# Fourteen places of a split operand, on one byte modulo 256 or on fourteen

## The chip, the core and the metric

The kernel runs on one core of one Trainium2 chip. The metric is the device time of one execution in microseconds; the median of several runs is given.

## What is computed

The input x has 2048 rows of 576 features. Two branches read it, an attention with memory and a gated feed-forward network, and a gate of x mixes them:

```
g = sigmoid((x * gate_w).sum(-1))
a = A(x, wq, wk, wv, wo, beta)      # 32 heads of 18, four segments of 512 rows:
                                    # causal softmax in a segment, mixed with a
                                    # running memory phi(k)^T v of the segments before
b = (silu(x @ w_gate) * (x @ w_up)) @ w_down      # 4608 hidden features
out = g * a + (1 - g) * b
```

## The kernel before

All large products are made of 4-byte operands that are split in two: a high part, rounded on ScalarE to the matmul's 4-byte format, and a low part, the difference, made on VectorE (`split`, lines 114 to 116). A product of two split matrices is three matmuls: high by high, high by low, low by high. TensorE loads one operand, 128 x 128, as weights and streams the other, up to 512 columns, past it.

The work comes in three stages.

The first stage (to about 225 us) runs over the four segments. For each, `qk` makes queries and keys by `products` (line 138): fourteen matmuls of 512 columns, in which weights of `qhi` and `qlo` are loaded and x's split parts stream. `v_step` makes the values by the same `products` with the parts exchanged: x's split parts are loaded as weights, and rows of `vw` stream.

The second stage (to about 1700 us) runs twice over 36 tiles of the hidden features, once for two of the segments and once for the other two. For a tile and two segments it needs gate and up projections; these are done with seven block products in place of eight (Strassen's scheme in Winograd's form), so seven calls of `seven(t, j)` for a tile. A call of `seven` is six matmuls of line 1034, with weights of a tile `wo_` and a stream of 512 columns of x's split part number j, and one of line 1037 for the last 64 features, with weights `rh` and the stream `xr`. There are 2 x 36 x 7 = 504 calls. Between the calls, `tick` and `beat` put other work: `down_group` (line 893, the down projection: streams of 320 or 256 columns of `dw`), and steps of the attention (lines 727 and 769 for the scores, 748 for a transposition, 798 and 800 for probabilities times values), all by a written order of steps.

The third stage multiplies the attention's result by wo (line 138 again, `wo` streams) and mixes the branches.

x's split operands lie in a pool `xo`, which is opened after the constants. It has fourteen places `x_slot(j, z)`, j from 0 to 6 and z 0 or 1, each with a high and a low part of 512 elements: [128, 2, 512] of 4 bytes, 4096 bytes in each partition. Place number n is 2j + z. In the first stage a segment's x lies in four of them, and the others serve as room for loads (`staging`): x's chunks, the weights of queries, keys and values, masks. Before the second stage the fourteen are filled with the seven combinations of x's blocks, two feature blocks each, `XO[j][z]` in place `SLOT[j]`, z; between the passes they are filled anew. In the third stage eight of them take loads of the feed-forward result. The same pool holds seven tiles `xr` of 2048 bytes.

Since 4096 and 2048 are multiples of 256, all fourteen places begin on the same byte modulo 256. Tiles `wo_` are 2048 bytes. The order of a call:

```
for z in range(2):
    for p, q in ((0, 0), (0, 1), (1, 0)):
        nc.tensor.matmul(t, w[:, p, z], x[z][:, q], ...)
nc.tensor.matmul(t, rem[:, RPOS[j]], XR[j], ...)
```

All DMAs are issued from SyncE (`nc.sync.dma_start`). The program reserves a ring for descriptors of dynamic DMAs in SBUF, here 1024 bytes (`dynamic_dma_scratch_size`, line 1221).

Of the kernel before, what the change touches and what calls it, by code (L numbers as in the profile page):

```python
# [20 lines left out]
P = 128  # L21
# [4 lines left out]
L = 512  # L26
# [27 lines left out]
RPOS = (0, 1, 4, 2, 5, 6, 3)  # L54
BLOCKS = {3: (4, 5), 6: (6, 7), 9: (8, 9), 12: (10, 11), 15: (12,), 18: (13,), 21: (14,), 24: (15,), 27: (16,), 30: (17,)}
KR = 6 * DH


def f32(ap):
# [4 lines left out]
def gated_mix(ctx, tc, xT, xrest, wf, wfr, wfh, wd, wv, wo, beta, cmask, ident, bmask, out):  # L64
    nc = tc.nc
    ctx.enter_context(tc.manual_schedule())

    def pool(st, name, bufs, side="left", space=None):
        if space is None:
            return st.enter_context(tc.tile_pool(name=name, bufs=bufs, side=side))  # L70
        return st.enter_context(tc.tile_pool(name=name, bufs=bufs, space=space))
# [24 lines left out]
    xo = pool(ctx, "xo", 1)  # L96
# [43 lines left out]
                mid()  # L140

    def x_slot(j, z, dtype=F32R):
        return xo.tile([P, 2, L], dtype, name=f"xo{j}{z}")

    def xr_tile(j, dtype=F32R):
        return xo.tile([P, L], dtype, name=f"xr{j}")
# [15 lines left out]
    def staging():  # L162
        return x_slot(*next(turns), F32).rearrange("p a b -> p (a b)")
# [11 lines left out]
    def stack_loads(u):  # L175
# [5 lines left out]
        for pr in range(2):  # L181
# [6 lines left out]
            if pr == 0:  # L188
                r += [(tq[5 * DH:KR], q[:, :, 2]), (tk[5 * DH:KR], k[:, :, 0])]
        return r  # L190

    def row_load(u):
        nc.sync.dma_start(qst[u % NST][KR:KR + 3].rearrange("z j (i n) -> z (j i) n", n=P), mxd[u])

# [75 lines left out]
    with ExitStack() as st:  # L270
# [18 lines left out]
        def x_tiles(s):  # L289
            j = 5 * (s % 2)  # L290
            return [x_slot(j + kt // 2, kt % 2) for kt in range(4)], xsp.tile([P, L], F32R, name="xs")
# [24 lines left out]
        def trio():  # L316
            ts = [first_tile() for _ in range(3)]
            xk, xs = xs_of[0]
            for kt in range(NT):
                nc.scalar.activation(qw[0][0][0][:, kt], qraw[kt][:, 0], AF.Copy)  # L320
                raw = xr[kt]
                if kt < 4:
                    split(xk[kt][:, 0], xk[kt][:, 1], raw)
                else:
                    xs_split(xs, raw)
                for m in range(3):
                    if m:
                        nc.scalar.activation(qw[m][0][0][:, kt], qraw[kt][:, m], AF.Copy)
                    nc.vector.tensor_sub(qw[m][1][0][:, kt], qraw[kt][:, m], f32(qw[m][0][0][:, kt]))
                for p, q in ((0, 0), (0, 1), (1, 0)) if kt < 4 else ((0, 0), (1, 0)):  # L330
                    for m in range(3):
                        nc.tensor.matmul(ts[m], qw[m][p][0][:, kt], xk[kt][:, q] if kt < 4 else xs,  # L332
                                         start=(kt == 0 and p + q == 0), stop=(kt == 4 and p == 1))
            return ts
# [128 lines left out]
        for kt in range(NT):  # L463
            if kt % 2 == 0:
                both = staging(), staging()
            a = both[0][:, L * (kt % 2):L * (kt % 2) + 3 * P].rearrange("p (m n) -> p m n", n=P)
# [14 lines left out]
        first = trio()  # L481
# [42 lines left out]
        def first_split(j, z):  # L524
            XO[j][z] = x_slot(SLOT[j], z)
            split(XO[j][z][:, 0], XO[j][z][:, 1], rx[{1: (0, z), 4: (1, z), 2: (1, 2 + z), 6: (0, 2 + z)}[j]])
# [155 lines left out]
    with ExitStack() as st:  # L682
# [37 lines left out]
        def s_bank(u, n):  # L720
# [4 lines left out]
            for c, pr, i in bank:  # L725
                w = P * (i + 1)
                nc.tensor.matmul(t[:, c:c + w], qs[:KR, pr, P * i:P * i + P], ks[:KR, pr, 0:w],  # L727
                                 start=True, stop=True)
# [34 lines left out]
        def t_bank(u, k):  # L763
            qs, ks = qst[u % NST], kst[u % NST]
            t = ts_tile()
            for pr, j in TPLAN[k]:
                _, c = blk(pr, j, j)
                w = L - P * j
                nc.tensor.matmul(t[:, c:c + w], ks[:KR + 3, pr, P * j:P * j + P], qs[:KR + 3, pr, P * j:L],  # L769
                                 start=True, stop=True)  # L770
# [271 lines left out]
        for pos, (half, f) in enumerate(seq):  # L1042
# [45 lines left out]
            a, y, xx = a_tile(), y_tile(), x_tile()  # L1088
# [63 lines left out]
        for n in range(17):  # L1152
# [6 lines left out]
            if n:  # L1159
                tt = order[n - 1]  # L1160
                ff = ffs.pop(n - 1)
                for hf in range(2):
                    c = slice(288 * hf, 288 * hf + 288)
                    t = chain_tile()
# [67 lines left out]
```

## Time and profile before

| what | value |
|---|---|
| median of 3 runs | 1804.82 us (1804.8 to 1804.99) |
| span of the profiled execution | 1803.0 us |
| TensorE busy | 1779.1 us, 99% |
| weight loads busy | 1529.7 us, 85% |
| VectorE, ScalarE, GpSimd busy | 1269.7, 960.0, 832.3 us |
| mean granted TensorE clock | 0.997 |
| DMA queue share | 60.3% |

The profile is one execution. Its page gives the span, from the first to the last instruction; the runs' times are 1.8 us above it. Busy time is the time in which an engine had an instruction under way; a matmul's length reaches to the modelled end of its pipeline, so lengths overlap, and the distance from one start to the next says more of the rate than a length does.

### The profile page before, as it was taken

To read this page: it belongs to the slowest core of one execution; us is meant where nothing else is said; L and a number is where in the kernel's file an instruction comes from. 1 tells how busy PE (TensorE), PEld (TensorE's weight loads), DVE (VectorE), ACT (ScalarE), POOL (GpSimd) and SP (SyncE) were. 2 spreads that over 40 slices of the span, in tenths; PEclk is the share of its full clock that TensorE was granted. 3 is DMA by queue.
4 is the path that set the end of the run, shared out by engine and by line. 5 is a ranking of instruction groups with operands and counts; after the bars stand their busy time and mean duration, and the time that the engine had idled before them with its cause. 6 is when DMAs were issued, how large, how long until landed. Compare 5 with 4: busy or idle time off the path is not lost.

```text
span 1803.0 us, 36363 instructions
## 1 busy us (share of the span) xinstructions
PE 1779.1 (99%) x12444; PEld 1529.7 (85%) x12444; DVE 1269.7 (70%) x3257; ACT 960.0 (53%) x1799; POOL 832.3 (46%) x1065
## 2 busy tenths in 40 slices
PE   9999999999999999999989999999999999999999
PEld 7898978888888888888877888888887887888899
DVE  6566566778877777777777767777777777764455
ACT  7666564465556555655546465355355355354511
POOL 4434632345554455345535555555555555553121
PEclk9999999999999999999999999999999999999999
DMA  8643496777657756776478456466455455456644
GB/s 289 215 174 141 148 324 205 229 260 264 186 198 248 256 181 193 246 247 193 160 262 247 137 176 195 135 172 195 124 179 181 144 168 180 137 160 187 199 137 139
DMA packets 244073, 352.01 MB, mean 195 GB/s; under 512 B 83440, under 2 KB 125680, under 8 KB 243888
## 3 DMA queue, kind: packets, MB, share of 16 engines
q1 hardware_dynamic: 243888, 349.68, 60.3%
q8 instruction: 99, 1.62, 0.4%
q14 instruction: 86, 0.70, 0.1%
HBM read 210.72 MB, written 138.87 MB: 194 GB/s over the span
## 4 chain that ended last, share of the span: by engine, by line
PE 92%; DVE 2%; DMA 2%; ACT 2%; issue 1%; SPq 0%; POOL 0%; ACTq 0%; DVEq 0%
PE bank L1034 36%; PE bank L893 25%; PE bank L138 11%; PE bank L1037 6%; PE bank L769 4%; PE bank L727 4%; PE bank L798 2%; PE bank L800 1%; PE bank L446 1%; PE bank L400 1%; DMA wo__23682<-wc 0%; DVE xo L116 0%; DMA stk<-q 0%; PE bank L332 0%; DMA raw<-in_xT_dram 0%
## 5 line engine op out<-in xcount | busy, mean ns | idle before, releaser
L893 PE MATMUL bank<-dw,hh 128*128 128x320 f32 (+1 forms) x2304 | 486.5, 304 | 6.0 <-DVE ya L898 4.4
L863 POOL TENSOR_TENSOR p<-pe,p 128x512 f16<-128x512 f32 x320 | 382.7, 1196 | 155.5 <-DVE p L861 107.1
L893 PEld LDWEIGHTS bank<-dw,hh 128*128 128x128 f32 x2304 | 377.9, 189 | 24.8 <-DVE ya L898 6.3
L773 ACT ACTIVATE pe<-bank 128x512 f32<-128x512 f32 x320 | 190.3, 595 | 313.9 <-PE bank L769 285.5
L893 PE MATMUL bank<-dw,hl 128*128 128x320 f32 (+1 forms) x1152 | 340.2, 295 | 0.3 <-DVE hl L116 0.3
L781 POOL TENSOR_SCALAR_AFFINE_SELECT pe<-pe 128x256 f32<-128x256 f32 (+1 forms) x320 | 137.5, 430 | 293.7 <-ACT pe L773 289.8
L734 DVE CUSTOM_DVE_ANT_0 scr<-bank,cm 128x512 bf16<-128x512 f32 (+3 forms) x512 | 247.8, 484 | 20.0 <-PE bank L727 12.0
L898 DVE TENSOR_TENSOR ya<-bank,ya 128x320 f32<-128x320 f32 x352 | 157.9, 453 | 113.2 <-PE bank L893 110.8
L893 PEld LDWEIGHTS bank<-dw,hl 128*128 128x128 f32 x1152 | 217.6, 189 | 0.9 <-DVE hl L116 0.9
L1037 PE MATMUL bank<-xr,rh 128*128 128x512 f32 x504 | 196.8, 391 | 0.0
L861 DVE CAST p<-pe 128x512 f16<-128x512 f32 x320 | 152.3, 476 | 0.0
L769 PE MATMUL bank<-qst,kst 111*128 111x512 bf16 (+3 forms) x512 | 150.9, 303 | 0.0
L727 PE MATMUL bank<-kst,qst 108*128 108x512 bf16 (+3 forms) x512 | 126.0, 300 | 0.6 <-DVE mb L734 0.5
L247 POOL TENSOR_TENSOR ws<-raw 128x256 f32<-128x256 f32 x72 | 66.2, 920 | 108.0 <-DMA raw<-in_wf_dram 51.7
L977 DVE TENSOR_TENSOR hl<-row,hh 128x512 fp32r<-128x512 f32 x120 | 99.7, 831 | 18.9 <-ACT hh L976 18.4
L1037 PEld LDWEIGHTS bank<-xr,rh 128*128 128x128 f32 x504 | 94.7, 188 | 20.3
L1101 ACT ACTIVATE row<-bank 128x512 f32<-128x512 f32 x72 | 43.1, 599 | 122.3 <-PE bank L1037 122.3
L1106 DVE TENSOR_TENSOR row<-bank,row 128x512 f32<-128x512 f32 x72 | 49.8, 691 | 81.8 <-ACT bank L1105 81.8
L1116 DVE TENSOR_TENSOR row<-bank,row 128x512 f32<-128x512 f32 x72 | 49.7, 690 | 64.2 <-PE bank L1037 51.5
L1105 ACT ACTIVATE bank<-bank 128x512 f32<-128x512 f32 x72 | 41.9, 582 | 97.9 <-PE bank L1037 94.8
L138 PE MATMUL bank<-xo,qhi 128*128 128x512 f32 x264 | 83.1, 396 | 0.0
L1098 DVE TENSOR_TENSOR bank<-bank,row 128x512 f32<-128x512 f32 x72 | 50.2, 697 | 41.6 <-PE bank L1037 33.4
(1702 smaller groups left out, 4040.3 us busy)
## 6 DMA issues: line engine op xcount, KB each, us to landing
rh<-rc SPq DMA_DIRECT2D x72, 336.0 KB
dc<-dw SPq DMA_DIRECT2D x36, 576.0 KB
dw<-dc SPq DMA_DIRECT2D x36, 576.0 KB
raw<-in_wf_dram SPq DMA_DIRECT2D x72, 256.0 KB
stk<-q SPq DMA_DIRECT2D x32, 384.0 KB
draw<-in_wd_dram SPq DMA_DIRECT2D x36, 288.0 KB
rc<-rt SPq DMA_DIRECT2D x42, 224.0 KB
vd<-vps SPq DMA_DIRECT2D x8, 912.0 KB
```

What stands on the lines that cost most here:

```text
L138: nc.tensor.matmul(t, st[n], mv[n], start=(n == 0), stop=(n == 13))
L727: nc.tensor.matmul(t[:, c:c + w], qs[:KR, pr, P * i:P * i + P], ks[:KR, pr, 0:w], start=True, stop=True)
L734: nc.vector.tensor_tensor_reduce(scr[:, :w], t[:, c:c + w], cm[:, L - w:L], 1.0, -3.0e38, OP.add, OP.max, m[:, k:k + 1])
L769: nc.tensor.matmul(t[:, c:c + w], ks[:KR + 3, pr, P * j:P * j + P], qs[:KR + 3, pr, P * j:L], start=True, stop=True)
L773: nc.scalar.activation(pe, t, AF.Exp, scale=SCALE)
L781: nc.gpsimd.affine_select(d, d, pattern=pat, compare_op=OP.is_ge, fill=0.0, base=0, channel_multiplier=-1)
L861: nc.vector.tensor_copy(p1, pe)
L863: nc.gpsimd.tensor_sub(p2, pe, p1)
L893: nc.tensor.matmul(t, p, q[:, cs], start=(n == 0), stop=(n == 3 * CH - 1))
L898: nc.vector.tensor_add(ya[:, i, cs], t, ya[:, i, cs])
L1034: nc.tensor.matmul(t, w[:, p, z], x[z][:, q], start=first and n == 0, stop=False, skip_group_check=True)
L1037: nc.tensor.matmul(t, rem[:, RPOS[j]], XR[j], start=False, stop=True, skip_group_check=True)
```

## The change

Each place gets padding, so that the fourteen begin on given bytes from the pool's beginning, beside the 4096 bytes of each place before it. The table `HOME` has these bytes; a tile is made larger by whole 32 bytes, and the remainder is an offset within it. The last entry, 768, is the sum of the padding. The ring of descriptors becomes 768 bytes smaller, 256 in place of 1024.

```
+HOME = (0, 40, 64, 128, 160, 216, 232, 264, 304, 352, 456, 504, 528, 544, 768)
...
     def x_slot(j, z, dtype=F32R):
-        return xo.tile([P, 2, L], dtype, name=f"xo{j}{z}")
+        n = 2 * j + z
+        first, after = HOME[n] // 32 * 32, HOME[n + 1] // 32 * 32
+        t = xo.tile([P, 2 * L + (after - first) // 4], dtype, name=f"xo{j}{z}")
+        a = HOME[n] % 32 // 4
+        return t[:, a:a + 2 * L].rearrange("p (a b) -> p a b", a=2)
...
-    nc = _bacc.Bacc("TRN2", target_bir_lowering=False, num_devices=1, dynamic_dma_scratch_size=1024)
+    nc = _bacc.Bacc("TRN2", target_bir_lowering=False, num_devices=1, dynamic_dma_scratch_size=256)
```

## The prediction

> **What bounds the kernel now.** I read the page first: the share of each engine, the DMA queues, the chain that ended last.
>
> ```profile
> span 1803.0 us, 36363 instructions
> ...
> PE 1779.1 (99%) x12444; PEld 1529.7 (85%) x12444; DVE 1269.7 (70%) x3257; ACT 960.0 (53%) x1799; POOL 832.3 (46%) x1065
> ...
> q1 hardware_dynamic: 243888, 349.68, 60.3%
> q8 instruction: 99, 1.62, 0.4%
> q14 instruction: 86, 0.70, 0.1%
> ...
> PE 92%; DVE 2%; DMA 2%; ACT 2%; issue 1%; SPq 0%; POOL 0%; ACTq 0%; DVEq 0%
> PE bank L1034 36%; PE bank L893 25%; PE bank L138 11%; PE bank L1037 6%; PE bank L769 4%; PE bank L727 4%; PE bank L798 2%; PE bank L800 1%; PE bank L446 1%; PE bank L400 1%; DMA wo__23682<-wc 0%; DVE xo L116 0%; DMA stk<-q 0%; PE bank L332 0%; DMA raw<-in_xT_dram 0%
> ```
>
> TensorE is busy 99% of the span and is 92% of the chain; line 1034, whose moving operand is x's split tile `xo`, is the largest part, 36%. So the time follows the pitch (start to start) of matmuls, and little else. The span is 1803.0 us, the median of the runs 1804.82 us: 1.8 us lie around the span, and I carry them over unchanged.
>
> Next the timeline of TensorE, for that pitch: columns are start, length from the first start to the last end, engine, line, operands, shape, count.
>
> ```profile
> 500.58 1.29 PE L1034 MATMUL bank<-xo,wo__6057 128*128 128x512 f32 x5
> 501.71 0.39 PE L1037 MATMUL bank<-xr,rh 128*128 128x512 f32 x1
> 501.94 1.52 PE L1034 MATMUL bank<-xo,wo__6070 128*128 128x512 f32 x6
> 503.30 0.39 PE L1037 MATMUL bank<-xr,rh 128*128 128x512 f32 x1
> 503.53 0.39 PE L1034 MATMUL bank<-xo,wo__6085 128*128 128x512 f32 x1
> ...
> 505.55 0.46 PE L893 MATMUL bank<-dw,hh 128*128 128x320 f32 x2
> 505.84 0.31 PE L893 MATMUL bank<-dw,hl 128*128 128x320 f32 x1
> 505.99 0.31 PE L893 MATMUL bank<-dw,hh 128*128 128x320 f32 x1
> ...
> 507.25 0.40 PE L893 MATMUL bank<-dw,hh 128*128 128x256 f32 x2
> 507.49 0.28 PE L893 MATMUL bank<-dw,hl 128*128 128x256 f32 x1
> 507.61 0.28 PE L893 MATMUL bank<-dw,hh 128*128 128x256 f32 x1
> ```
>
> One call of `seven` is seven products, from 501.94 to 503.53: 1.59 / 7 = 227 ns each, no idle time between. Three products of 320 columns take 505.99 - 505.55 = 0.44 us, 147 ns each; three of 256 take 0.36, 120 ns each. The difference, 27 ns for 64 columns, is 0.417 ns for a column. So 512 columns account for 213.3 ns, 320 for 133.3 and 256 for 106.7, and each of the three widths carries about the same rest: 13.8 (the row's 10 ns stand behind it), 13.3, 13.3. I use 13.3, and 226.7 ns for the pitch at 512. The change can act on that rest alone, and only where it depends on the byte at which an operand starts.
>
> Does it depend on that? Two more places of the timeline.
>
> ```profile
> 507.97 1.55 PE L1034 MATMUL bank<-xo,wo__6092 128*128 128x512 f32 x6
> ...
> 208.09 1.74 PE L138 MATMUL bank<-vw,xo 128*128 128x288 f32 x12
> 209.67 0.43 PE L138 MATMUL bank<-vw,xs 128*128 128x288 f32 x2
> 209.94 0.83 PE L446 MATMUL bank<-Mm,ph 128*128 128x152 f32 x6
> ...
> 1101.65 0.38 PE L727 MATMUL bank<-kst,qst 108*128 108x512 bf16 x1
> 1101.87 0.27 PE L769 MATMUL bank<-qst,kst 111*128 111x256 bf16 x1
> ```
>
> The six products at 507.97, the first after another kind of matmul, span 1.55 us where the six at 501.94 span 1.52: the same code, operands on the same bytes, so the rest also has a memory of what went before and takes some products to settle. The fourteen products of `v_step` from 208.09 to 209.94 have moving operands that start on other bytes: a row of `vw` is 290 elements, 1160 bytes, so its five chunks begin on 0, 136, 16, 152 and 32 modulo 256, and the low halves on others. They take 1.85 / 14 = 132.1 ns; their 288 columns account for 120, so the rest is 12.1 where the products on one byte carry 13.3. And a bf16 product of 512 columns has a pitch of 0.22 us, a rest of 5 to 7 ns. The rest is thus no fixed cost of the array; it is smaller for other operands, and only a little smaller where 4-byte operands are spread.
>
> **The change part by part.** Nothing is added or removed in instructions; the matmuls, loads, copies and DMAs are the same in number and order. Three things move.
>
> *The byte of the moving operand.* Each place of `xo` was 4096 bytes, so all fourteen began on one byte modulo 256. Now they begin 0, 40, 64, 128, 160, 216, 232, 8, 48, 96, 200, 248, 16 and 32 bytes further modulo 256 (the table, reduced). The places grow by 768 bytes in all, which is what the ring gives up, and 768 is three times 256: every other tile keeps its byte modulo 256, and the products of lines 893, 798, 800, 727 and 769 keep theirs. Touched are 504 calls of `seven` (line 1037 has one product in each, x504 on the page):
>
> ```profile
> L1037 PE MATMUL bank<-xr,rh 128*128 128x512 f32 x504 | 196.8, 391 | 0.0
> ...
> L138 PE MATMUL bank<-xo,qhi 128*128 128x512 f32 x264 | 83.1, 396 | 0.0
> ...
> L138 PE MATMUL bank<-xo,qlo 128*128 128x512 f32 x132 | 51.6, 391 | 0.0
> ```
>
> That is 6 x 504 = 3024 products of line 1034 and 396 of line 138, 3420 with `xo` as moving operand, of 12444. Bounds for one: at best the rest falls to that of the bf16 product, 13.3 to about 5, a gain of 8 ns, 27 us over all. At worst no product ever settles, because each meets another pair of bytes than the one before: the 1.55 us span has five pitches and one length of 0.39, (1.55 - 0.39) / 5 = 232 ns, 5.3 ns above 226.7, 18 us over all. The nearest row is that of `v_step`, also 4-byte operands, a moving operand on changing bytes and weights on one: 12.1, a gain of 1.2 ns. I take that: 3420 x 1.2 = **-4.1 us**.
>
> A rule of the Trainium skill speaks against any effect: "TensorE: Matmul & The Clock Gate", section "Step-by-step: what each phase is for", says that TensorE reads SBUF through two independent ports, one for the streamed operand and one for the weights, so that a weight load takes no read bandwidth from the running matmul. By it the bytes could not matter to this pair and the term would be nothing; the trace's 12.1 against 13.3 does not bear that out fully, but does not refute it either, since widths and weights differ there as well.
>
> *The settling.* The second pass has 252 calls of `seven`, most of them behind other matmuls. One that settles costs 0.03 us more (1.55 against 1.52), so at most 252 x 0.03 = 7.6 us are in it, and fewer, since some calls follow one another. If the pitch differs from product to product anyway, the slow run after a switch should lose its regular form; I take the unsettled part as two thirds of that, 5 us, and credit half of it, **-2.5 us**, with ends at 0 and -7.6.
>
> *Loads into the places.* x's chunks, the weights of the first stage and, at the end, the attention's partner `ffd` are loaded by DMA into places of `xo` that start off 32 or 64 bytes now.
>
> ```profile
> 2.31 4.90 DMA xo<-in_xT_dram
> ...
> xo<-in_xT_dram SPq DMA_DIRECT2D x20, 256.0 KB
> ```
>
> One such load is on the chain, 4.90 us at the start; the others lie beside TensorE, which waits for them nowhere in its list of waits. Between nothing and a tenth of that load: **+0.2 us**, ends 0 and +0.5. The Trainium skill, "DMA: Bandwidth & Descriptors", section "How a descriptor splits into AXI transactions", says that a transfer which does not begin on 256 bytes pays one more transaction; for a row of 2048 bytes that is nine in place of eight, by which this load would be an eighth longer, an estimate of 0.6 us. No row of this trace shows a load off its alignment.
>
> *The ring.* All but 185 of the packets are on the queue `hardware_dynamic`, the 185 are instructions, and all DMAs are issued on SP; no queue of GpSimd appears. The ring of descriptors is in use by none of them: 0, and there is no row by which a smaller one could cost.
>
> ACT's and DVE's copies into the places keep shape and count; the engines are at 53% and 70%, and hide a few ns each behind TensorE; without that cover a copy of 16 in the first stage would cost its own lengthening only. Sum: -4.1 - 2.5 + 0.2 = -6.4 us. Span 1796.6, time **1798.4 us**. For this case alone I give 1789 to 1801: the settling and the rest between one half of and twice what I took, and somewhat beyond.
>
> **The rivals.**
>
> *Never settled (slower).* On one byte the products reach 227 ns and stay there for dozens of calls; that steady pitch is a property of a relation that repeats, and with fourteen bytes it never repeats for more than three products. Then the mean is the unsettled 232 ns. The first pass, mostly settled now, loses most. For it: 1.55 against 1.52 with equal bytes. Against it: `v_step` changes bytes at almost every product and is not slower. Price: 5.3 x 3420 = 18 us less the 5 us that are unsettled already: +13 us, 1818 us, from 1809 to 1823. It decides if the mean pitch of the calls that follow one another passes 228 ns.
>
> *No effect.* The rest of 13.3 ns belongs to the weight load's hand-over and not to bytes; the three widths with equal rests speak for it. Time 1804.8, within 0.2% (3.6 us, 1 ns a product), which is about what a measurement of this kernel can tell from no change.
>
> *The collision goes.* The rest falls to the bf16 product's 5 to 7 ns in most products: 3420 x 7 = 24 us, 1781 us. For it: that row. Against it: `v_step`, spread and still at 12.1. By the rule "Back-to-back issue gap" of the same page of the Trainium skill, N / 2.4 + 2.5, the pitch could be 215.8 ns; no 4-byte product here comes near it.
>
> **How the numbers follow.** Forecast (modest gain) 0.43, collision goes 0.09, no effect 0.19, never settled 0.29. Faster by over 0.2%: 0.43 + 0.09 = 0.52; within: 0.19; slower: 0.29. The range leaves out the collision case below 1784 (0.09) and the upper end of the slower case above 1821 (about 0.1): 1784 to 1821.
>
> **What would show it.** In settled calls of the first pass: six products of line 1034 and one of 1037 spanning on the mean under 1.58 us (1.59 now), with single pitches no longer all equal; 1.60 or more is the slower rival, an unchanged 1.59 everywhere the rival of no effect, 1.54 the collision that goes. `v_step`'s fourteen at 1.85 us should move less than 0.03, lines 893 at 147 and 120 ns not at all; if those move too, the byte of `xo` is not what acts. DVE, ACT and POOL busy sums should stay within 1%. The forecast is wrong if the mean pitch of line 1034 in the first pass is unchanged or higher while the time still falls, or if a wait for a DMA into `xo` shows on TensorE.

## The result, and the profile after

The changed kernel is slower: 1819.27 us median of three runs (1816.74 to 1819.37) against 1804.82, a ratio of 1.0076 with a 95% interval from 1.006 to 1.0093, or +14.45 us. The profiled execution of the changed kernel took 1819.27 us itself, 1817.5 us of it span. Three executions among those of the experiments below were slow (one of e1_ring, one of e6_one and one of the kernel before beside e4_both), and the medians here leave them out. The lines of code have moved up by one to five numbers there: 1034, 1037, 893 and 138 are now 1039, 1042, 898 and 139.

The page of the changed kernel: the span, busy time of each engine, and the chain that ended last. PE is TensorE, PEld its weight loads, DVE VectorE, ACT ScalarE and POOL GpSimd.

```profile
span 1817.5 us, 36363 instructions
...
PE 1796.2 (99%) x12444; PEld 1534.4 (84%) x12444; DVE 1271.3 (70%) x3257; ACT 960.6 (53%) x1799; POOL 832.4 (46%) x1065
...
PE 92%; DVE 3%; ACT 1%; DMA 1%; issue 1%; POOL 1%; SPq 0%; DVEq 0%; ACTq 0%; POOLq 0%
```

The instructions are as many as before, and DVE, ACT and POOL are as busy as before to 0.2%. TensorE alone has grown, from 1779.1 to 1796.2 us. So the time is lost in TensorE's matmuls. The `...` in the block stands for lines left out, here and below. The timeline of TensorE of the changed kernel (start, length, engine, line, operands, shape, count), in calls of `seven` shortly ahead of those shown of before, and in the same call of `v_step`:

```profile
498.25 1.58 PE L1039 MATMUL bank<-xo,wo__5964 128*128 128x512 f32 x6
499.67 0.39 PE L1042 MATMUL bank<-xr,rh 128*128 128x512 f32 x1
499.89 1.56 PE L1039 MATMUL bank<-xo,wo__5970 128*128 128x512 f32 x6
501.29 0.39 PE L1042 MATMUL bank<-xr,rh 128*128 128x512 f32 x1
501.52 1.56 PE L1039 MATMUL bank<-xo,wo__5986 128*128 128x512 f32 x6
...
209.91 1.75 PE L139 MATMUL bank<-vw,xo 128*128 128x288 f32 x12
211.51 0.42 PE L139 MATMUL bank<-vw,xs 128*128 128x288 f32 x2
211.77 0.82 PE L451 MATMUL bank<-Mm,ph 128*128 128x152 f32 x6
```

From 498.25 to 499.89 and on to 501.52 are 1.64 and 1.63 us for seven products, 1.59 before. Most calls look like this: among the calls of both passes that stand between other calls the median is 1628 ns, against 1587 before, so 232.6 ns a product in place of 226.7. The products no longer settle at 226.7; most starts are 224 to 238 ns apart, and the same pattern comes back in tile after tile. The products with 288 columns, which load `xo` as weights, take 1.86 us for fourteen, 1.85 before.

The same by groups of instructions (busy time, mean ns of one, idle before), the changed kernel first and then the kernel before:

```profile
L898 PE MATMUL bank<-dw,hh 128*128 128x320 f32 x1152 | 265.2, 317 | 5.1 <-DVE ya L903 3.7 <-ACT hh L116 1.3
L898 PE MATMUL bank<-dw,hh 128*128 128x256 f32 x1152 | 224.9, 291 | 0.8 <-DVE ya L903 0.7
L1042 PE MATMUL bank<-xr,rh 128*128 128x512 f32 x504 | 197.9, 393 | 0.0
L139 PE MATMUL bank<-xo,qhi 128*128 128x512 f32 x264 | 84.0, 399 | 0.0
L139 PE MATMUL bank<-xo,qlo 128*128 128x512 f32 x132 | 52.2, 395 | 0.0
```

```profile
L893 PE MATMUL bank<-dw,hh 128*128 128x320 f32 x1152 | 265.0, 316 | 5.2 <-DVE ya L898 3.7 <-ACT hh L115 1.4
L893 PE MATMUL bank<-dw,hh 128*128 128x256 f32 x1152 | 224.5, 291 | 0.8 <-DVE ya L898 0.7
```

The down projection, whose operands did not move against each other, costs the same. The queries' and keys' products with `xo` (`qhi`, `qlo`) have grown by 0.9 and 0.6 us, and the rest is line 1039. Summed from each start to the next, line 1034/1039 went from 715.6 to 728.5 us (+13.0) and the 432 products of x's places with `qhi` and `qlo` (lines 138 and 332, now 139 and 337) from 101.3 to 102.9 (+1.6): together 14.6 us, as much as the whole loss.

### The profile page after: what moved, and what is told of

It reads as the page before. It is cut to its first block, busy times and chain, and to the rows that moved or that the text cites. A ratio compares the mean times of both kernels' runs of the same rounds, so it can differ in the third digit from the quotient of the medians.

```text
span 1817.5 us, 36363 instructions
## 1 busy us (share of the span) xinstructions
PE 1796.2 (99%) x12444; PEld 1534.4 (84%) x12444; DVE 1271.3 (70%) x3257; ACT 960.6 (53%) x1799; POOL 832.4 (46%) x1065
## 3 DMA queue, kind: packets, MB, share of 16 engines
q8 instruction: 99, 1.62, 0.4%
## 4 chain that ended last, share of the span: by engine, by line
PE 92%; DVE 3%; ACT 1%; DMA 1%; issue 1%; POOL 1%; SPq 0%; DVEq 0%; ACTq 0%; POOLq 0%
PE bank L1039 37%; PE bank L898 24%; PE bank L139 10%; PE bank L1042 6%; PE bank L774 4%; PE bank L732 4%; PE bank L803 2%; PE bank L805 1%; PE bank L405 1%; DVE xo L117 1%; PE bank L451 1%; PE bank L337 1%; DMA stk<-q 0%; PE bank L957 0%; DMA raw<-in_xT_dram 0%
```

## The experiments

All edits are against the changed kernel unless the text says otherwise; ratios are to the kernel before on the same chip. The experiments were made on the view that in the kernel before all operands of the 4-byte 512-column products, streams (`xo`, `xr`) and weights (`wo_`, `rh`, `qhi`, `qlo`) alike, lie on one byte modulo 256, and that the change moved the streams `xo` alone. No trace holds addresses; the runs bear it out, since the kernel's products settle at the pitch that equal bytes have in m1_bytes, and moving `xo`, `xr` or `rh` alone by 128 bytes costs time.

**e1_ring: the small ring, without the fourteen bytes.**

```
-HOME = (0, 40, 64, 128, 160, 216, 232, 264, 304, 352, 456, 504, 528, 544, 768)
+HOME = 14 * (0,) + (768,)
```

> The ring of 256 bytes alone: the table is fourteen zeros and 768, so the padding lies behind the last place, all fourteen places stay on one byte modulo 256, and all other tiles are where the changed kernel has them. Theory 'change of byte' (a product settles at a pitch of 227 ns while the starting bytes of its operands repeat, and every change of byte from one product to the next throws it off): 1804.8 us, pitch 227 ns. Rival 'relation to the weights' (x off the byte of its weights costs by itself, repeated or not): 1804.8 too. Rival 'ring' (the smaller ring or the moved constants cost): about 1819.

Measured: 1803.72 us against 1803.71; 1.0002 [0.9992, 1.0011]. The ring and the shift of the constants cost nothing; the loss is in the bytes.

**e2_shift: all fourteen on one byte, but another one than the weights'.**

```
+    xo.tile([P, 32], F32, name="gap2")
...
+HOME = 14 * (0,) + (640,)
```

> All fourteen places on one byte, but 128 bytes from the byte of the weights, of xr and of the rest (a tile of 128 bytes ahead of the first place, 640 behind the last). 'Change of byte': the six products of a call repeat their relation, and only the product with xr differs, so two changes in seven products: between 1804.8 and 1812. 'Relation to the weights': 3420 products pay, as much as with fourteen bytes or more: 1819 or above. Rival 'fine alignment' (only starts off a multiple of 32 bytes cost): 1804.8.

Measured: 1814.18 us; 1.0059 [1.0044, 1.0074], +10.5 us. The time lies between the two expectations. Here nothing differs from product to product in the six, yet nearly three quarters of the loss are there. Timeline of TensorE of this kernel:

```profile
495.13 1.55 PE L1040 MATMUL bank<-xo,wo__5971 128*128 128x512 f32 x6
496.52 0.39 PE L1043 MATMUL bank<-xr,rh 128*128 128x512 f32 x1
496.75 1.54 PE L1040 MATMUL bank<-xo,wo__5987 128*128 128x512 f32 x6
```

1.62 us a call; the median of the calls that stand between others is 1623 ns, 231.9 ns a product. It is not the variety of bytes alone that costs.

**e3_by32: fourteen different bytes, all multiples of 32.**

```
+HOME = tuple(range(0, 448, 32)) + (768,)
```

> The fourteen places 32 bytes further from one to the next, so eight bytes modulo 256, all multiples of 32: the bytes change as often as in the changed kernel. 'Change of byte': about as slow as the changed kernel, 1815 to 1822. 'Fine alignment': 1804.8, since no place starts off 32 bytes. 'Relation to the weights': 1815 to 1822.

Measured: 1817.64 us; 1.0083 [1.0066, 1.0099]. The median call takes 1629 ns, 232.7 ns a product. The places that begin off 32 bytes are not the cause.

**m1_bytes: 512-column products alone.** Rows of matmuls on two tiles, `xm` as stream and `wm` as weights, with the starting bytes `a` and `w`, counted from the beginning of the tile; nothing else runs, and the reference's computation is left out.

```
for k, (a, w) in enumerate(run):
    o = 128 * (k % 4) + w // 4
    nc.tensor.matmul(t, wm[:, o:o + P], xm[:, a // 4 + 512 * (k // 4 % 2):a // 4 + 512 * (k // 4 % 2) + 512],
...
```

> Not the kernel's computation: matmuls of 128 x 512 in the 4-byte format alone, one after the other, 26 to 98 in a group, in which only the starting bytes of the streamed operand and of the weights are set. Its total time says nothing; read is the pitch. Groups: streamed operand on byte 0, 8, ... 248 with weights on 0; weights on 0, 8, ... 248 with the stream on 0; both moved together; the stream's byte switched by d every three products, and every product; four groups in the order of the calls of seven with the table of the changed kernel, with zeros, with the table rounded down to 32, and with steps of 32. 'Change of byte': each of the first 72 groups settles at 226 to 227 ns whatever the byte, the switched ones and the table of the changed kernel stay above, at 230 to 234 on the mean. 'Relation to the weights': the settled pitch rises with the distance of the two bytes, to 232 and more. 'Fine alignment': it rises at starts off 32 bytes only.

The timeline of TensorE of this kernel has one line for each row; here are stream on 128 with weights on 0, both on 0, both on 128, the changed kernel's fourteen bytes in the order of its calls, and the same with fourteen zeros:

```profile
110.55 6.31 PE L59 MATMUL bank<-xm,wm 128*128 128x512 f32 x26
...
211.29 6.18 PE L59 MATMUL bank<-xm,wm 128*128 128x512 f32 x26
...
442.34 6.19 PE L59 MATMUL bank<-xm,wm 128*128 128x512 f32 x26
...
618.75 23.06 PE L59 MATMUL bank<-xm,wm 128*128 128x512 f32 x98
...
641.78 22.50 PE L59 MATMUL bank<-xm,wm 128*128 128x512 f32 x98
```

A row begins unsettled, so I take the last twelve pitches of a row of 26. With equal bytes (0, 32, 64, 96 or 128 on both sides) the pitch settles at 226.7 ns. With the weights on 0 and the stream on any of 31 other bytes the last twelve are 228.9 to 236.6 in the mean, 233.0 over all, in no order of the distance; with the stream on 0 and the weights elsewhere the mean is 232.0, 16 of 31 at 233.3, and three bytes (120, 144, 240) reach 226.7. Equal bytes off 32 give 230.8 (8), 231.25 (168, 200) and 233.3 (16). Rows in which the stream's byte changes at every product or every third have means of 230 to 237. Behind its first fourteen products the changed kernel's table gives 232.6, and zeros give 226.7. So the two kernels' pitches, 232.6 and 226.7, come out of TensorE's products alone, with no other engine and no DMA at work.

**e4_both: x and `wo_` both 128 bytes further, `xr` and `rh` left.**

```
+HOME = 14 * (0,) + (128,)
+    xo.tile([P, 32], F32, name="gap2")
...
                     rhs.append(wop.tile([P, 7, P], F32R, name=f"rh{z}", bufs=1))
+                wop.tile([P, 32], F32, name="gapa", bufs=1)
...
+        wop.tile([P, 32], F32, name="gapb", bufs=1)
```

> The shifted kernel again, all fourteen places 128 bytes off, but now the tiles wo_, the weights of line 1034, are moved by 128 bytes as well, so that in a call of seven x's parts and their weights are on one byte again; xr and rh, and all the rest, stay where they were. Theory 'relation to the weights': the 3024 products of line 1034 return to the pitch of before, only the 396 of line 138 (x against qhi and qlo) stay off, 396 times 6.7 ns = 2.6 us, and one product in seven meets another byte: 1804 to 1809. 'Change of byte': the changes between x and xr are those of the shifted kernel, so 1814 as there.

Measured: 1814.49 us against 1802.89; 1.0069 [1.0051, 1.0087]. The time did not come back. I had expected six products of seven to be cured. Timeline of TensorE of this kernel:

```profile
495.46 1.55 PE L1042 MATMUL bank<-xo,wo__5973 128*128 128x512 f32 x6
496.85 0.39 PE L1045 MATMUL bank<-xr,rh 128*128 128x512 f32 x1
497.08 1.56 PE L1042 MATMUL bank<-xo,wo__5989 128*128 128x512 f32 x6
```

1.62 us for these calls; the median over all calls between others is 1632 ns, 233.1 ns a product. They don't settle, though in five of seven the stream, its weights and the weights loaded beside it have equal bytes. One product in seven whose stream and weights both stayed behind keeps the other six unsettled.

**m2_widths: the same products alone, at other widths.** As m1_bytes, with 256 to 512 columns; the reference's computation is left out.

```
for i, (n, run) in enumerate(RUNS):
...
    nc.tensor.matmul(t[:, :n], wm[:, o:o + P], xm[:, c:c + n], ...)
```

> Not the kernel's computation: matmuls alone as in the probe of bytes, with 256, 288 and 320 columns and the streamed operand or the weights on byte 0, 8, ... 248, and with 352 to 512 columns for eight bytes. Read is the settled pitch, by the number of columns and the distance of the bytes. If 'relation to the weights' holds for every width, the rest beyond 0.4167 ns a column is 13.3 on one byte and 17 to 23 off it for all widths, and the products of v_step, at 12.1, need another reason. If it holds for long streams alone, the rest off the byte at 288 columns lies near 12, as in v_step, and grows with the columns; then the prediction's row was taken from a width at which spreading costs nothing.

Rows of 24 in its timeline of TensorE, in pairs: 256 columns on equal bytes and with the stream on 192; 288 on equal bytes and with the stream on 128; 512 on equal bytes and with the stream on 128:

```profile
22.61 3.12 PE L44 MATMUL bank<-xm,wm 128*128 128x256 f32 x24
...
96.80 3.00 PE L44 MATMUL bank<-xm,wm 128*128 128x256 f32 x24
...
121.36 3.41 PE L44 MATMUL bank<-xm,wm 128*128 128x288 f32 x24
...
176.09 3.45 PE L44 MATMUL bank<-xm,wm 128*128 128x288 f32 x24
```

```profile
868.71 5.71 PE L44 MATMUL bank<-xm,wm 128*128 128x512 f32 x24
...
897.60 5.84 PE L44 MATMUL bank<-xm,wm 128*128 128x512 f32 x24
```

Over 23 pitches the other byte costs 0.13 us at 512 columns (5.7 ns each), 0.04 at 288 (1.7 ns), and at 256 it gains 0.12 (5.2 ns). In the settled rest beyond 0.4167 ns a column: 512 columns 13.3 on equal bytes, mean of the others 19.5; 320 columns 13.3 and 14.0; 288 columns 11.7 and 12.9; 256 columns 13.3 and 12.1 (6.7 to 20.0). The widths differ in what the byte does, and some relation at 256 columns is better than the equal one. (At 512 columns seven other bytes of the stream were taken, at 256 to 320 columns 31 of the stream and 31 of the weights.) With seven other bytes of the stream at 352, 384, 416, 448 and 480 columns, the rests are 14.4, 13.3, 15.0, 16.0 and 16.7 on equal bytes, and the best other byte gives 11.7 at 352 and 13.3 at the rest. Equal bytes are the best, or level with the best, at 384 and 512 columns alone; the mean of the others lies 6.2 ns above them at 512 and at most 1.8 at the other widths.

**e5_all: all four operands of a call 128 bytes further.** The places and `xr` are moved by the tile `gap2` ahead of them, `rh` and `wo_` by `gapa`; `gap3` and `gapb` keep what follows.

```
+HOME = 15 * (0,)
+    xo.tile([P, 32], F32, name="gap2")
+    pool(ctx, "gap3", 1).tile([P, 32], F32, name="gap3")
...
                 wraw_of[0] = [w_load(0, u) for u in range(2)]
+                wop.tile([P, 32], F32, name="gapa", bufs=1)
                 for z in range(2):
                     rhs.append(wop.tile([P, 7, P], F32R, name=f"rh{z}", bufs=1))
...
+        wop.tile([P, 32], F32, name="gapb", bufs=1)
```

> All operands of a call of seven moved together: the fourteen places, xr, wo_ and rh all 128 bytes further, and nothing else. Theory 'equal bytes, undisturbed' (a product of 512 columns settles at 227 ns when the stream starts on the byte, modulo 256, of the weights that are loaded beside it, and only after some ten such products in a row; one pair in seven that differs is enough to keep it unsettled): the calls are back at 227 ns, and only the 396 products of line 138 stay off, at most 2.6 us: 1803 to 1807, against 1814 with xr and rh left behind. If a moved byte costs by itself, or the rows of other tiles matter: 1810 or above.

Measured: 1803.24 us against 1803.91; 0.9994 [0.9984, 1.0003]. Timeline of TensorE of this kernel:

```profile
492.44 1.52 PE L1044 MATMUL bank<-xo,wo__5957 128*128 128x512 f32 x6
493.80 0.39 PE L1047 MATMUL bank<-xr,rh 128*128 128x512 f32 x1
494.03 1.52 PE L1044 MATMUL bank<-xo,wo__5971 128*128 128x512 f32 x6
```

1.59 us a call again, 1587 ns in the median. The 432 products with `qhi` and `qlo`, whose weights stayed, pay still (103.1 us from start to start, 101.3 in the kernel before). The byte itself is free; what counts is that streams and weights of the whole sequence agree.

**e6_one: one place of fourteen 128 bytes off.**

```
+HOME = 4 * (0,) + (128,) + 9 * (256,) + (768,)
```

> Of the fourteen places one alone, number 4 (j = 2, z = 0), is 128 bytes off; all others are where the kernel before has them. If the cost goes by the products whose stream is off: 3 of 42, a fourteenth of 14 us, 1804 to 1806. 'Equal bytes, undisturbed': the three products and the ten or so after them are unsettled, some 13 of 49 at 5 ns, 65 ns in each of 72 tiles: 4.7 us, 1807 to 1811.

Measured: 1806.28 us against 1803.91; 1.0013 [1.0004, 1.0022], +2.4 us, between the two expectations. Timeline of TensorE of this kernel, a call whose first three products stream that place, the call behind it, and a later one without it:

```profile
480.28 1.55 PE L1039 MATMUL bank<-xo,wo__5567 128*128 128x512 f32 x6
481.67 0.40 PE L1042 MATMUL bank<-xr,rh 128*128 128x512 f32 x1
481.90 1.53 PE L1039 MATMUL bank<-xo,wo__5651 128*128 128x512 f32 x6
483.27 0.39 PE L1042 MATMUL bank<-xr,rh 128*128 128x512 f32 x1
...
489.84 1.52 PE L1039 MATMUL bank<-xo,wo__5950 128*128 128x512 f32 x6
491.20 0.39 PE L1042 MATMUL bank<-xr,rh 128*128 128x512 f32 x1
```

The call with the place takes 1.62 us from start to start, the two others 1.59. The three products on the other byte have pitches of 234, 224 and 238 ns, and a tail follows (230, 235, 229, 232, then 231 and back at 227): some 40 ns in each of 72 tiles, 2.9 us. So the step leaves about five more products unsettled; it isn't remembered for a whole tile.

**e7_dw: only the down projection's stream `dw` on another byte** (192 further; xo as in the kernel before), for the gain that m2_widths showed at 256 columns.

```
+HOME = 14 * (0,) + (512,)
...
         r = fp.tile([P, D], F32, name="draw", bufs=1)
+        if not gapd:
+            gapd.append(fp.tile([P, 48], F32, name="gapd", bufs=1))
...
+        pool(st, "gap3", 1).tile([P, 16], F32, name="gap3")
         yp = pool(st, "yp", 1)
```

> The places of x as in the kernel before (all on one byte), ring of 256; instead the tiles dw, the stream of the down projection (line 893), are moved by 192 bytes, the distance at which the probe of widths settled at a rest of 6.7 ns in place of 13.3 for 256 columns and stayed at 13.3 for 320. If the probe carries over: the 1728 products of 256 columns fall from 120 to 113 ns, up to 11.5 us less, 1793 to 1800; if nine products in a row are too few to settle, less of it, down to nothing; and if the products of line 1034 behind each group are thrown off, up to 3 us more, 1804 to 1808.

Measured: 1800.26 us against 1803.91; 0.9979 [0.997, 0.9988], −3.65 us, and so faster than both kernels. Timeline of TensorE of this kernel:

```profile
506.01 0.40 PE L902 MATMUL bank<-dw,hh 128*128 128x256 f32 x2
506.24 0.28 PE L902 MATMUL bank<-dw,hl 128*128 128x256 f32 x1
506.36 0.40 PE L902 MATMUL bank<-dw,hh 128*128 128x256 f32 x2
506.60 0.28 PE L902 MATMUL bank<-dw,hl 128*128 128x256 f32 x1
```

Three products take 0.35 us against 0.36 before; from the trace's starts a product of 256 columns went from 120 to 117 ns, their sum from 221.1 to 218.2 us, most of the gain, and those of 320 columns stayed at 147. The long rows of the measurement alone had promised 113 ns; in the kernel not more than about nine of these products follow each other before the width changes.

**e8_xr: only `xr` 128 bytes off**, the stream of the seventh product.

```
+HOME = 14 * (0,) + (128,)
+    pool(ctx, "gap3", 1).tile([P, 32], F32, name="gap3")
```

> x's fourteen places, the weights and all else as before; only xr, the stream of the seventh product of a call (line 1037), starts 128 bytes off. If the cost goes by the products whose stream is off, 504 of them at some 5 ns: 2.5 us, 1805 to 1808. 'Equal bytes, undisturbed': one product in seven is enough to keep the other six from settling, so most of the 504 calls pay as in the shifted kernel, where two pairs in seven or five differed: 1811 to 1816.

Measured: 1806.91 us against 1804.18; 1.0018 [1.0009, 1.0028], +2.7 us. Timeline of TensorE of this kernel:

```profile
489.31 1.52 PE L1041 MATMUL bank<-xo,wo__5954 128*128 128x512 f32 x6
490.67 0.40 PE L1044 MATMUL bank<-xr,rh 128*128 128x512 f32 x1
490.90 1.52 PE L1041 MATMUL bank<-xo,wo__5968 128*128 128x512 f32 x6
```

Only the seventh product pays: 234 ns from its start to the next, and the six stay at 227. The 1811 to 1816 us that go with six disturbed products were not there. A single stream on another byte, then, leaves no tail, unlike the three in e6_one.

**e9_rh: only `rh` 128 bytes off**, the weights of the seventh product.

```
+HOME = 14 * (0,) + (256,)
+                wop.tile([P, 32], F32, name="gapb", bufs=1)
                 for z in range(2):
                     rhs.append(wop.tile([P, 7, P], F32R, name=f"rh{z}", bufs=1))
+                wop.tile([P, 32], F32, name="gapa", bufs=1)
```

> The mirror of the run with xr: all streams and wo_ as before, only rh, the weights of the seventh product of a call, start 128 bytes off. The stream of the sixth product then runs beside a weight load off its byte, and the seventh product's stream beside wo_ as before. If weights off the byte cost like a stream off it, by the product alone: 504 at 6 to 7 ns, 3 us, 1805 to 1809, the other products of calls that follow one another at 227. If one weight load off the byte leaves the following products unsettled (as would explain why the calls with x and wo_ moved and xr and rh left behind do not settle at all): 1811 to 1816, with pitches of 228 to 238 all through the call.

Measured: 1807.69 us against 1804.15; 1.0023 [1.0013, 1.0033], +3.5 us. Timeline of TensorE of this kernel:

```profile
488.84 1.53 PE L1041 MATMUL bank<-xo,wo__5952 128*128 128x512 f32 x6
490.20 0.40 PE L1044 MATMUL bank<-xr,rh 128*128 128x512 f32 x1
490.44 1.53 PE L1041 MATMUL bank<-xo,wo__5966 128*128 128x512 f32 x6
```

Now the sixth product pays too (232, the seventh 234), the one beside whose stream `rh` is loaded; the other five stay at 227. Neither `xr` nor `rh` alone disturbs the whole call, so e4_both isn't explained by one foreign operand in seven; there, stream and weights moved together.

**m3_calls: the calls' patterns with matmuls alone.** As m1_bytes; six products and a seventh with the bytes of e2, e8, e9 and e4, and rows of equal products with one step in them; the reference's computation is left out.

```
def calls(six, one, n=8):
    return ([six] * 6 + [one]) * n
...
for d in (32, 64, 128, 192):
    RUNS += [calls((d, 0), O), calls(O, (d, 0)), calls(O, (0, d)), calls((d, d), O), calls((0, d), O)]
```

> Not the kernel's computation: matmuls of 512 columns alone again, in the pattern of calls (six of one kind and one of another, eight times), for d = 32, 64, 128, 192: six streams off by d; the seventh stream off; the seventh weights off; six with both stream and weights moved by d; six weights off. Then a row of 14 on one byte, followed by one stream off, three streams off, one weight load off, or a lasting move of both or of the stream. If the patterns alone make the pitches of the kernel's runs, d = 128 gives 231 to 233 ns for six streams off, 227.6 for the seventh stream, 228.6 for the seventh weights, and, the open point, 232 to 233 for both moved though every product has its own two operands on one byte. In the rows: if a move of both operands together disturbs, the products after it take several to come back to 227; if only unequal bytes count, at most one or two products differ. A last group has the fourteen bytes of the changed kernel with the weights on the same bytes: 227 if only unequal bytes count, above 230 if the moves do.

The rows for 128 bytes in its timeline of TensorE, in the order of the code: six streams off, the seventh's stream off, the seventh's weights off, six both off.

```profile
157.28 13.20 PE L53 MATMUL bank<-xm,wm 128*128 128x512 f32 x56
...
170.46 13.00 PE L53 MATMUL bank<-xm,wm 128*128 128x512 f32 x56
...
183.43 13.05 PE L53 MATMUL bank<-xm,wm 128*128 128x512 f32 x56
...
196.46 13.24 PE L53 MATMUL bank<-xm,wm 128*128 128x512 f32 x56
```

At a settled pitch 56 would span 55 x 0.2267 + 0.39 = 12.86 us. Over the last six calls of a row the means are 231.0, 227.6, 228.6 and 232.4 ns, and the four kernels' medians are 231.9, 227.6, 228.6 and 233.1: the order of all four, and their sizes to 0.9 ns, come out of the bytes alone, the surprise of e4_both among them. That surprise is strongest at 128: with 32, 64 and 192 bytes, six both off give 229.3, 230.5 and 229.5. Six weights off by 128 give 232.4, no less than streams.

In the rows with one step, one stream on 128 costs one product of 233 and nothing after it; three on 128 run at 234, 225 and 237 and leave a tail of 230, 235, 229, 233 and 231, which is e6_one's call almost to the nanosecond; one on 32 makes ten products unsettled, itself included, one on 64 eight (236, 241, 224, 231, 236, 228, 233, 231), one on 192 six; weights alone on 128 for one product lengthen the product before it (232), beside which they are loaded, and then 233 and 228; a joint move by 128 that lasts takes three products (232, 230, 228) to settle again; a stream that stays on 128 stays unsettled, 233.4 in the mean. Three products on each of the changed kernel's fourteen bytes, with the weights on the same byte as the stream, have 232.6 behind the first fourteen products: in this row it does not help to move the weights along.

## Why the prediction was wrong, point by point

The time of 1819.27 us lies within the stated 1784 to 1821, which took in the slower rival, but not within the 1789 to 1801 of the forecast's own case, and it moved the other way: +14.45 us where −6.4 was forecast.

What bounds the kernel: right. The whole loss appears as pitch of TensorE's products with `xo`, and nothing else grew. The count of these products, 3420, left out 36 of line 332, about 1%.

*The byte of the moving operand, −4.1 us: this step failed, with its sign.* It took −1.2 ns a product from the row of `v_step` as the nearest one, 12.1 ns of rest on changing bytes at 288 columns against 13.3 on one byte at 512. m2_widths shows what was wrong in it: 288 columns have a rest of 11.7 on equal bytes already, so the 12.1 were that width's own and no gain from the spread; and the byte moves the rest by 1.2 ns in the mean at 288 columns but by 6.2 at 512. Rests that agree at three widths, as the prediction observed, were on this view all on equal bytes, and say nothing about how they react to others. In its place stand +13.0 us in line 1039 and +1.6 in lines 139 and 337. The prediction's own worst case (232 ns, read off the unsettled 1.55 us span) was the right size: 232.6 measured. Those 5.9 ns over 226.7 would be 20 us for 3456 products; 14.6 were lost, since products behind other matmuls were unsettled already.

*The settling, −2.5 us: wrong too.* It reasoned that the slow run after a switch loses its form when every product differs. In fact a product that meets other bytes is about as slow as an unsettled one, and in most rows of m3_calls makes the next ones so. In the 232 calls that come right behind other matmuls, the second to the sixth product take 1154 ns together in the kernel before and 1163 in the changed one (medians): no gain there either.

*Loads and ring: right* as far as they can be told. e1_ring puts the ring at nothing (1.0002), and TensorE's list of waits has no new DMA. The 0.2 us for the loads is too small to be seen in runs that differ by 2 us. ScalarE's copy that waits for the load on the chain begins at 7.24 us before and at 7.13 in the changed kernel, so that neither this term nor the estimate of 0.6 us beside it shows; that estimate counts a transaction that is filled in part like a full one.

*The rival "never settled", given 0.29, is what happened*: 1818 us forecast, 1819.27 measured, with the point that it named (over 228 ns in the calls that follow each other). Its reason was only half the matter. It blamed a relation that never repeats; e2_shift repeats one and still loses 10.5 us, since a constant difference between stream and weights doesn't settle at 226.7 either, and e5_all repeats equal bytes elsewhere and loses nothing. What spoke against it, `v_step`, was evidence from the wrong width.

*No effect (0.19)* fell with m1_bytes: the rest isn't a fixed hand-over. So did what the prediction drew, in its step on the byte, from the rule of the Trainium skill in "TensorE: Matmul & The Clock Gate", section "Step-by-step: what each phase is for", that the two reads of SBUF go through ports of their own. Two separate ports may be there, and no run here tells; but the starting bytes of the two operands are not independent in time, 226.7 ns against 233.3 with the stream on 128 and nothing else running. *The collision goes (0.09)*: no relation that was tried brings a 512-column product below 226.7; a rest as low as 6.7 ns was found at 256 columns alone, in long rows (e7_dw gained 3 ns a product by it).

The marks were well chosen: calls at 1.63 us (1.60 or more named the slower rival), `v_step` moved by 0.01, lines 893 stayed, the other engines' sums within 0.2%.

What stays open is the mechanism inside TensorE: why many unequal bytes share one pitch, 233.3, and a few have 226.7, why a joint move of stream and weights in six products of seven keeps all unsettled (e4_both) where either operand alone doesn't (e8_xr, e9_rh), and why some steps leave a tail. The rows give the prices, not the reason. That it is the weights loaded beside a stream which count, and not those in use, is suggested by the sixth product in e9_rh and by the row with one step of the weights, but no run separates the two fully.

## What to carry to other kernels

Where 4-byte products of 512 columns follow each other, give the streams, their weights and those of the products between them one and the same byte modulo 256, a multiple of 32; at other widths measure first, since of the other widths that were measured the equal byte was as good as any at 384 columns alone. Spreading places, harmless as it looks in counts and busy shares of other engines, cost 2.6% of the pitch here. A price taken from rows of another width can have the wrong sign: when the mechanism is unknown, let the worst row of the same shape carry the forecast, or measure rows of the instruction alone at that very shape. For 256 columns the best byte is another one, and in a short group it yields only a part of what a long row promises (117 ns in place of 113).

## What the runs showed of the hardware that was not expected

- 512-column products of 4-byte operands settle at 226.7 ns when stream and weights begin on equal bytes modulo 256 that are multiples of 32, and run at 229 to 237 ns, 25 of 62 rows at 233.3, when the bytes differ; three unequal relations (weights on 120, 144 and 240) reach 226.7 too. This holds with nothing else running.
- TensorE has a memory over products: one product whose stream is off by 32 or 64 bytes makes eight to ten run unsettled (224 to 241 ns), itself included; one off by 128 leaves nothing after it.
- Equal bytes off a multiple of 32 do not settle fully: 230.8 ns on 8, 231.25 on 168 and 200, 233.3 on 16.
- The effect depends on width: 6.2 ns in the mean at 512 columns, 1.2 at 288, 0.7 at 320, and −1.2 at 256, where two offsets of the stream, 112 and 192, leave a rest of 6.7 instead of 13.3. At 416, 448 and 480 columns equal bytes leave 15.0, 16.0 and 16.7, and another byte of the stream 13.3.
